# Seven block products in place of eight for the output matrix of a gated feed-forward block

## The chip, the cores and the metric

The kernel runs on one core of one Trainium2 chip. The metric is the device time of one execution in microseconds (us); lower is better. Before the change it is 1617.84 us, the median of three runs (1617.23 to 1620.64). In the profile, PE is the matrix engine (TensorE), PEld its loading of the stationary operand, DVE is VectorE, ACT is ScalarE, POOL is GpSimd and SP the engine that issues most transfers.

## The reference

Two blocks run one after the other, in 32-bit floating point.

```python
# q, k, v: (8 batches, 8 heads, 576 positions, 64)
scores = scale * q @ k^T
scores = where(scores >= max(scores) - tau, scores, -1e9)
attn   = exp(scores - max) / (sum + 1e-9)
x      = (attn @ v)                      # heads side by side: 4608 tokens x 512
g      = x @ w_gate                      # 4608 x 1536
out    = (g * sigmoid(g) * (x @ w_val)) @ w_out      # 1536 -> 512
```

The change concerns the last product, `hidden @ w_out`, in which `hidden` is the gated 4608 x 1536 array.

## The kernel before

The 4608 tokens are cut into units of 256. For a unit, `gate` and `value` form two rows of 128 hidden features at a time on PE (8 matmuls with 256 moving columns each). `value` multiplies them on DVE; `sigmoids` then applies the sigmoid on ACT and the second multiplication on POOL. It does so for three such pairs at a time (`SIG = 3`), so a unit of six pairs needs it twice. A pair lies in a tile `ht` of 128 x 2 x 256: 128 features, two of them side by side, 256 tokens. `output` multiplies the finished tiles with `w_out`, 128 tokens at a time: twelve matmuls with 512 moving columns, in the order of the features, so that the tiles are read from the first to the last.

```python
def value(j, cs, f, hts, gts):
    ps = rows_of_products(j, cs, f, 1, "pv")                                          # PE
    nc.vector.tensor_tensor(out=hts[f // 2][:, :, 0:n], in0=gts[...], in1=ps, op=ALU.mult)   # DVE, L471
    ...
def sigmoids():
    for _, gt, own in unsig:
        nc.scalar.activation(gt, gt, AF.Sigmoid)                                      # ACT, L480
        for x, ht in enumerate(own):
            nc.gpsimd.tensor_tensor(out=ht, in0=ht, in1=gt[:, 2*x:2*x+2, :], op=ALU.mult)    # POOL, L482
    unsig.clear()

def output(tiles):                       # tiles: (unit, 128-token half)
    for (j, lo, hi), i in tiles:
        po = ps_f.tile([P, 512], ...)
        for f in range(NF):              # NF = 12
            if f % OF == 0:              # OF = 3
                if any(u[0] is hts for u in unsig):
                    sigmoids()
            nc.tensor.matmul(po, hts[f//2][:, f%2, i*P:(i+1)*P], wo[:, f, :], ...)    # PE, L497
            ...                          # after the last f: copy on ACT, transfer out
            if f % OF == OF - 1:
                yield OCOST
```

The products of a unit come late: four pieces into the next unit if there is one, and at once if none is ready.

```python
def block():
    late = iter(())
    while True:
        if not ready:
            yield from late              # no next unit yet: the outputs at once
            ...
        unit = ready.popleft()
        for f in range(0, NF, GR):       # GR = 2
            if f == EARLY:               # EARLY = 4
                yield from late
            gate(...);  yield c
            value(...); yield c
        late = output(tiles_of(unit))
```

All of this fills the gaps of the attention part. Attention goes by slots: a batch has four pairs of heads with five slots each. A slot forms scores on PE, takes maxima on DVE, exponentials on ACT, masks them on DVE, and divides by the sums on POOL (`p`, L327). Two slots later DVE transposes the divided `p` in `turn` (L342); the masks of that later slot come after this in DVE's order, and the scores of the slot after it wait for those masks. Between the steps `fill(part)` issues pieces of the feed-forward block, at a rate that `pace` sets. It is the smallest of the averages, taken up to each coming supply of units, of work over slots.

```python
for x, t in enumerate(seg["tiles"]):
    go = scores(seg, t)
    next(go)                 # scores on PE, maxima on DVE, exponentials on ACT
    ...
    next(go)                 # turn(1) and the masks on DVE
    fill(part)
    next(go)                 # exchange of the sums on ACT
    if len(unsig) >= SIG:
        sigmoids()
    fill(part)
    next(go)                 # sums on DVE, the division of p on POOL
    ...
```

The 64 last positions of each batch make two further units of 256 tokens. The first of them is worked in two halves of 128 tokens, one after the second batch and one after the fourth.

Of the kernel before, what the change touches and what calls it, by code (L numbers as in the profile page):

```python
# [2 lines left out]

# [6 lines left out]
F32 = mybir.dt.float32  # L10
# [3 lines left out]
ALU = mybir.AluOpType  # L14
# [4 lines left out]
def kernel(  # L19
# [25 lines left out]

    nc = tc.nc
    P = 128
    B, H, S, D = q.shape  # L50
    NP = H // 2
    DM, DFF = w_gate.shape
    NCC = DM // P
# [8 lines left out]
    NT = SM // P  # L62
    SH = S // 2
    TC = 256
    XB = 6
    NU = SM // TC
    BT = TC // (S - SM)
    NPAIR = B * NP
    TA = 2
    QA = TA * P  # L70
# [3 lines left out]
    const = ctx.enter_context(tc.tile_pool(name="const", bufs=1))  # L74
    ld = ctx.enter_context(tc.tile_pool(name="ld", bufs=1))
    qkp = ctx.enter_context(tc.tile_pool(name="qkp", bufs=2))
    ptp = ctx.enter_context(tc.tile_pool(name="ptp", bufs=2))
    stp = ctx.enter_context(tc.tile_pool(name="stp", bufs=4))
    hp = ctx.enter_context(tc.tile_pool(name="hp", bufs=8))
    gp = ctx.enter_context(tc.tile_pool(name="gp", bufs=5))  # L80
# [22 lines left out]
    make_identity(nc, ident)  # L103
    vall = const.tile([P, 2 * NJ * D], F32, name="vall")

    wgv = const.tile([P, 2, NCC, DFF], F32, name="wgv")
    wo = const.tile([P, NF, DM], F32, name="wo")

    FW = 384
    TW = 2 * FW  # L110
    spare = const.tile([P, 2 * TW], F32, name="spare")


    XW = NCC * TC
    xall = const.tile([P, XB * XW], F32, name="xall")

    hfirst = const.tile([P, NF, TC], F32, name="hfirst")

# [8 lines left out]
    land = wo.rearrange("p f e -> p (f e)")  # L129
    places = [land[:, n * 2 * TW:(n + 1) * 2 * TW] for n in range(NF * DM // (2 * TW))]  # L130
    places += [xall[:, 3 * XW + n * 2 * TW:3 * XW + (n + 1) * 2 * TW] for n in range(2)]
    los = deque(spare[:, n * TW:(n + 1) * TW] for n in range(2))
    for f in range(0, DFF, FW):
        for c in range(NCC):
            wpieces.append((wgv[:, :, c, f:f + FW], [w[c * P:(c + 1) * P, f:f + FW] for w in (w_gate, w_val)],
# [116 lines left out]
    def scores(seg, t):  # L252
        qT, kT, tiles, halved = seg["qT"], seg["kT"], seg["tiles"], seg["halved"]
        if halved and "p" not in seg:
            seg["p"] = ptp.tile([P, 2 * NT + 1, S], F32, name="p")
        q0 = t * P - seg["q0"]
        heads = [slice(h * D, (h + 1) * D) for h in range(2)]
        if t < NT:
            pss = [ps_s.tile([P, 2, 512], F32, name="sc") for _ in range(2)]
            at = [tiles.index(t), len(tiles) + tiles.index(t)]  # L260
        else:
            pss = [ps_s.tile([P, 2, 512], F32, name="sc")]
            at = [tiles.index(t)]
        if halved:
            put = [(pss[h], u, h, q0 + u * D) for u in range(2) for h in range(2)] if t < NT else \
                [(pss[0], h, h, q0) for h in range(2)]
# [200 lines left out]
    def value(j, cs, f, hts, gts):  # L467
        n = cs.stop - cs.start
        per = rows_per(n)
        ps = rows_of_products(j, cs, f, 1, "pv")  # L470
        nc.vector.tensor_tensor(out=hts[f // 2][:, :, 0:n], in0=gts[f // per][:, f % per:f % per + GR, :], in1=ps,  # L471
                                op=ALU.mult)
        if f % per == per - GR:
            unsig.append((hts, gts.pop(f // per), [hts[x][:, :, 0:n] for x in range((f + GR - per) // 2, f // 2 + 1)]))
        if f == NF - GR and cs.stop == TC:
            del xts[j]

    def sigmoids():
        for _, gt, own in unsig:
            nc.scalar.activation(gt, gt, AF.Sigmoid)  # L480
            for x, ht in enumerate(own):
                nc.gpsimd.tensor_tensor(out=ht, in0=ht, in1=gt[:, 2 * x:2 * x + 2, :], op=ALU.mult)  # L482
        unsig.clear()

    SIG = NF // 4
    OF = 3

    def output(tiles):
        for (j, lo, hi), i in tiles:
            hts = hidden[j, lo, hi]  # L490
            po = ps_f.tile([P, 512], F32, name="po", tag="psf")[:, 0:DM]
            for f in range(NF):
                if f % OF == 0:
                    if any(u[0] is hts for u in unsig):
                        sigmoids()
                    need(NCC * DFF // FW + DM // ne * (f * P // FW + 1))
                nc.tensor.matmul(po, hts[f // 2][:, f % 2, i * P:(i + 1) * P], wo[:, f, :],  # L497
                                 start=(f == 0), stop=(f == NF - 1))
                if f == NF - 1:
                    ob = op.tile([P, DM], F32, name="ob")  # L500
                    nc.scalar.copy(ob, po)  # L501
                    kind, at = j
                    if kind == "full":
                        b, u = divmod(at, NU)
                        at = b * S + u * TC + i * P
                        nc.gpsimd.dma_start(out=out[at:at + P, :], in_=ob)  # L506
                    else:
                        for x in range(2):
                            at = (j[1] * BT + lo // D + 2 * i + x) * S + SM
                            nc.gpsimd.dma_start(out=out[at:at + D, :], in_=ob[x * D:(x + 1) * D, :])  # L510
                if f % OF == OF - 1:
                    yield OCOST

    EARLY = 4
    HCOST, OCOST = NCC, OF * DM / TC
    hidden = {}
    ready = deque()

    def tiles_of(unit):

        first, second = (("full", 0), 0, TC), (("full", 1), 0, TC)
        units = [] if unit == first else [first, second] if unit == second else [unit]
        return [(u, i) for u in units for i in range((u[2] - u[1]) // P)]

    def cost(unit):
        return 2 * NF * HCOST * (unit[2] - unit[1]) / TC + len(tiles_of(unit)) * NF / OF * OCOST

    def supply(b):  # L530

        got = [(("full", b * NU + u), 0, TC) for u in range(NU)]
        if b < BT and b % 2:
            got.append((("last", 0), b // 2 * P, (b // 2 + 1) * P))
        elif b >= BT and b % BT == BT - 1:
            got.append((("last", b // BT), 0, TC))
        return got

    left = [0.0]

    def block():
        late = iter(())
        while True:
            if not ready:
                yield from late
                if not ready:
                    yield 0
                continue
            unit = ready.popleft()
            j, lo, hi = unit  # L550
            cs = slice(lo, hi)
            hts, gts = hidden.setdefault(unit, {}), {}
            c = GR * HCOST * (hi - lo) / TC
            for f in range(0, NF, GR):
                if f == EARLY:
                    yield from late
                gate(j, cs, f, hts, gts)
                yield c
                value(j, cs, f, hts, gts)
                yield c  # L560
            late = output(tiles_of(unit))

    pieces = block()
    credit = [0.0]
# [1 line left out]
    def fill(n):  # L566

        credit[0] += n
        while credit[0] > 0:
            c = next(pieces)  # L570
            left[0] -= c
            credit[0] = credit[0] - c if c else 0
            if not c:
                return 0
        return 1

    def start_batch(b):
        def place(n):
            return xall[:, n * XW:(n + 1) * XW].rearrange("p (c t a r) -> p c t a r", c=NCC, a=2, r=G)

        half = XB // 2
        for u in range(NU):
            j = b * NU + u
            while ("full", j - 2 * NU) in xts:
                fill(HCOST)
            xts["full", j] = place(b % 2 * half + u)
        if b % BT == 0:
            xts["last", b // BT] = place(b // BT % 2 * half + NU)

    arenas = [ptp.tile([P, 2 * NT + 1, S], F32, name="p") for _ in range(2)]
    early = list(range(TA))
    rest = list(range(TA, NT + 1))
    flat = [x.rearrange("p n s -> p (n s)") for x in arenas]
    pbufs = deque(arenas[1][:, 2 * x:2 * x + 2] for x in range(2))
    pTbufs = deque(flat[1][:, 2 * x * S:(2 * x + 2) * S] for x in range(2, 4))
    segs = [{"i": i, "tiles": early, "halved": False} for i in range(NP)]
    segs += [{"i": i, "tiles": rest, "halved": False} for i in [NP - 1, *range(NP - 1)]]  # L600
    segs += [{"i": i, "tiles": list(range(NT + 1)), "halved": True} for i in range(NP, NPAIR)]
    assert (2 * KT + 1) * P <= 2 * S and NP + 4 <= 2 * NT
    gains = []
    for n, seg in enumerate(segs):
        seg["gives"] = supply(n // NP - 1) if n % NP == NP - 1 and n >= NP else []
# [27 lines left out]
    def prepare(seg):  # L633

        i = seg["i"]
        if i in kept:
            seg.update(kept[i])
            return
        qr, kr = raws[i]
        kept[i] = None  # L640
        qT = qkp.tile([P, S], F32, name="qT")
        if i < NP:
            kT = arenas[0][:, 4 + i, :]
            rest = flat[0][:, i * (S - QA):(i + 1) * (S - QA)]
            nc.vector.transpose(out=kT, in_=kr)
            nc.vector.transpose(out=qT[:, 0:QA], in_=qr[:, 0:QA])
            nc.vector.transpose(out=rest, in_=qr[:, QA:S])
            kept[i] = {"kT": kT, "qT": rest, "q0": QA}
        else:
            kT = qkp.tile([P, S], F32, name="kT")  # L650
            nc.vector.transpose(out=kT, in_=kr)
            nc.vector.transpose(out=qT, in_=qr)
        seg.update(kT=kT, qT=qT, q0=0)
# [103 lines left out]
```

## Time and profile before

| | |
|---|---|
| Median time | 1617.84 us |
| Span of the profiled execution | 1615.6 us |
| PE busy | 1546.1 us (96%) |
| DVE busy | 996.4 us (62%) |
| POOL busy | 779.7 us (48%) |
| ACT busy | 710.7 us (44%) |
| Attention ends at about | 1410 us |

A busy PE here means that some matmul was under way; matmuls overlap a little at their ends, so rates are better taken from the starts of following groups. A group of instructions in the profile is named by its line in the kernel, its engine and its operation, with the written tile left of the arrow. Every 32-bit matmul leaves two records in this trace, so `x16` stands for eight matmuls. An entry such as `[1.03 <-POOL ht L482]` says that the engine stood idle for 1.03 us before the row and that line 482 on POOL ended the wait.

### The profile page before, as it was taken

Reading aid. Unit: us, or ns where it says so; the run is one execution under the profiler, and the core shown is the slowest. Engines: PE = TensorE matmul, PEld = TensorE weight load, DVE = VectorE, ACT = ScalarE, POOL = GpSimd, SP = SyncE. Lnnn points to the kernel's source line nnn. Section 1 sums busy time; section 2 is a strip of 40 time slices with the busy share of each in tenths; the row PEclk is TensorE's granted clock in tenths of the full one; section 3 lists DMA queues with packets and bytes.
Section 4 is the critical chain, followed back from the end, with each engine's and each line's share of the span. In section 5 each row is a group of like instructions: output and inputs, shape, how many; then the busy total and the mean of one; then the engine's idle time right before and its main releaser. Section 6 shows DMA issues by size and latency. Waiting matters only on the chain.

```text
span 1615.6 us, 30135 instructions
## 1 busy us (share of the span) xinstructions
PE 1546.1 (96%) x11344; PEld 1031.3 (64%) x11344; DVE 996.4 (62%) x3058; ACT 710.7 (44%) x1864; POOL 779.7 (48%) x726
## 2 busy tenths in 40 slices
PE   6898879899999999999999999999999999999998
PEld 4675555357575775657666766676755775577865
DVE  6886877776667766666666767666666677500000
ACT  6776754334444444444444444444444354311110
POOL 3554466554555555455555455554646554511111
PEclk9899989999999999999999999999999999999999
DMA  7541221111111111011111111101111110000000
GB/s 171 139 142 56 77 50 31 43 43 31 37 37 44 31 37 37 19 34 29 31 43 37 37 37 30 44 13 32 31 43 37 37 33 27 1 14 7 7 14 13
DMA packets 176417, 66.84 MB, mean 41 GB/s; under 512 B 159632, under 2 KB 159632, under 8 KB 176272
## 3 DMA queue, kind: packets, MB, share of 16 engines
q1 hardware_dynamic: 173328, 55.47, 15.2%
q0 software_dynamic: 2944, 9.44, 1.7%
q8 instruction: 90, 1.47, 0.4%
q14 instruction: 55, 0.45, 0.1%
HBM read 55.44 MB, written 9.44 MB: 40 GB/s over the span
## 4 chain that ended last, share of the span: by engine, by line
PE 80%; DVE 7%; ACT 2%; issue 1%; POOL 1%; POOLq 0%; DVEq 0%; ACTq 0%
PE po L497 21%; PE pv L451 21%; PE pg L451 21%; PE sc L272 9%; PE xa L409 8%; DVE p L312 2%; DVE mx L292 1%; DVE p L342 1%; DVE mx L247 1%; POOL p L327 1%; ACT p L308 1%; DVE wo L185 0%; ACT L308 0%; DVE wo L183 0%; DVE wo L181 0%
## 5 line engine op out<-in xcount | busy, mean ns | idle before, releaser
L327 POOL TENSOR_SCALAR p<-p,ri 128x288 f32<-128x288 f32 x486 | 479.0, 1001 | 290.6 <-DVE ri L322 248.7
L451 PE MATMUL pg<-xall,wgv 128*128 128x256 f32 (+1 forms) x1824 | 401.8, 373 | 5.6 <-POOL wgv L190 5.6
L451 PE MATMUL pv<-xall,wgv 128*128 128x256 f32 (+1 forms) x1824 | 398.8, 372 | 0.0
L451 PEld LDWEIGHTS pg<-xall,wgv 128*128 128x128 f32 x1824 | 330.6, 191 | 75.2 <-issue 19.4
L451 PEld LDWEIGHTS pv<-xall,wgv 128*128 128x128 f32 x1824 | 330.2, 191 | 59.7 <-issue 13.6
L497 PE MATMUL po<-wo,ht 128*128 128x512 f32 x816 | 364.0, 598 | 1.0 <-POOL ht L482 1.0
L312 DVE SCALAR_TENSOR_TENSOR p<-sc,th,p 128x288 f32<-128x288 f32 (+1 forms) x540 | 258.5, 529 | 57.3 <-ACT p L308 56.4
L497 PEld LDWEIGHTS po<-wo,ht 128*128 128x128 f32 x816 | 151.2, 190 | 192.0 <-issue 182.9
L482 POOL TENSOR_TENSOR ht<-ht,gt 128x512 f32<-128x512 f32 (+1 forms) x108 | 127.9, 1211 | 226.5 <-ACT gt L480 210.9
L308 ACT ACTIVATE p<-sc,nm 128x288 f32<-128x288 f32 (+1 forms) x540 | 236.8, 511 | 0.7
L292 DVE TENSOR_REDUCE mx<-sc 128x2 f32<-128x576 f32 x252 | 179.3, 748 | 73.3 <-PE sc L272 69.9
L471 DVE TENSOR_TENSOR ht<-gt,pv 128x512 f32<-128x512 f32 (+1 forms) x108 | 70.8, 655 | 232.4 <-PE pv L451 227.4
L304 ACT ACTIVATE th<-nm,cut 128x4 f32<-128x4 f32 (+1 forms) x140 | 41.6, 297 | 391.6 <-DVE nm L295 391.5
L272 PE MATMUL sc<-kT,qT 64*32 64x288 f32 x4032 | 170.8, 413 | 27.3 <-DVE p L312 27.1
L342 DVE STREAM_TRANSPOSE p<-p 128x576 f32<-128x576 f32 x252 | 181.3, 753 | 2.2 <-POOL p L327 2.2
L250 ACT COPY sums<-sums 32x4 f32<-32x4 f32 (+1 forms) x560 | 108.5, 194 | 137.4 <-DVE p L312 130.0
L272 PEld LDWEIGHTS sc<-kT,qT 64*32 64x32 f32 x4032 | 66.5, 106 | 120.5 <-issue 93.3
L409 PE MATMUL xa<-p,vall 64*64 64x288 f32 x2016 | 130.6, 409 | 8.7 <-issue 6.3
L409 PEld LDWEIGHTS xa<-p,vall 64*64 64x64 f32 x2016 | 79.2, 134 | 59.8 <-issue 17.0
L465 ACT COPY gt<-pg 128x512 f32<-128x512 f32 (+1 forms) x114 | 64.7, 567 | 112.0 <-PE pg L451 111.5
L506 POOL DMA_DIRECT2D out_dram<-ob x32 | 19.3, 603 | 171.3 <-ACT ob L501 169.0
L247 DVE TENSOR_REDUCE mx<-mx 32x4 f32<-32x4 f32 (+1 forms) x560 | 83.2, 149 | 10.4
(78 smaller groups left out, 962.5 us busy)
## 6 DMA issues: line engine op xcount, KB each, us to landing
vall<-in_v_dram SPq DMA_DIRECT2D x112, 144.0 KB, 3.1
qraw<-in_q_dram SPq DMA_DIRECT2D x128, 72.0 KB, 2.3
kraw<-in_k_dram SPq DMA_DIRECT2D x128, 72.0 KB, 2.7
out_dram<-ob POOLq DMA_DIRECT2D x32, 256.0 KB, 2.4
wo<-in_moe_w_gate_dram SPq DMA_DIRECT2D x16, 384.0 KB, 3.5
wo<-in_moe_w_val_dram SPq DMA_DIRECT2D x16, 384.0 KB, 4.1
xall<-in_moe_w_out_dram SPq DMA_DIRECT2D x6, 768.0 KB, 4.6
wo<-in_moe_w_out_dram SPq DMA_DIRECT2D x2, 768.0 KB, 4.3
```

Of the source, the lines that this page charges most:

```text
L247: nc.vector.tensor_reduce(out=out, in_=in_, axis=AX.X, op=ALU.max)
L250: nc.scalar.copy(out, in_[:, :, 0])
L272: nc.tensor.matmul(ps[g * G:(g + 1) * G, u, 0:SH], qT[hs, col + a * G:col + (a + 1) * G], kT[hs, c * SH:(c + 1) * SH], start=True, stop=True)
L292: nc.vector.tensor_reduce(out=mx[:, 2 * x:2 * x + 2, 0], in_=tile_[:, :, 0:SH], axis=AX.X, op=ALU.max, negate=True)
L308: nc.scalar.activation(ps[x], scs[x], AF.Exp, bias=nm[:, x:x + 1])
L312: nc.vector.scalar_tensor_tensor(out=ps[x], in0=scs[x], scalar=th[:, x:x + 1], in1=ps[x], op0=ALU.is_ge, op1=ALU.mult, accum_out=sm[:, x, ...
L327: nc.gpsimd.tensor_scalar(out=ps[x], in0=ps[x], scalar1=ri[:, x:x + 1], scalar2=None, op0=ALU.mult)
L342: nc.vector.transpose(out=p, in_=p)
L409: nc.tensor.matmul(xa[a][h * D:(h + 1) * D, at:at + n * G].rearrange("d (i q) -> d i q", q=G), vr[rs, h, j, :], p[rs, lo:lo + n, j, :], st ...
L451: nc.tensor.matmul(ps[:, i], wgv[:, mat, c, (f + i) * P:(f + i + 1) * P], x[:, c, cs], start=(c == 0), stop=(c == NCC - 1))
L482: nc.gpsimd.tensor_tensor(out=ht, in0=ht, in1=gt[:, 2 * x:2 * x + 2, :], op=ALU.mult)
L497: nc.tensor.matmul(po, hts[f // 2][:, f % 2, i * P:(i + 1) * P], wo[:, f, :], start=(f == 0), stop=(f == NF - 1))
```

## The change

A unit's output is a product of a 256 x 1536 matrix with a 1536 x 512 matrix. Cut into two by two blocks, it takes eight block products; Strassen's method takes seven, at the price of sums of blocks. Four sums of blocks of `w_out` are formed once on POOL (`sums_of_weights`). The sums of blocks of the hidden array are formed per unit on POOL, in `sigmoids` and in `seven`. The sums of the products go to DVE, with one on POOL. The first two units keep the old `output`. To make room, the two attention buffers `p` overlap by two tiles, with the slots of odd pairs of heads in another order, and the last tokens have one place in place of two. The first of their units is then worked as a whole, after the fourth batch and ahead of that batch's other units.

```diff
     def sigmoids():
-        for _, gt, own in unsig:
+        for hts, gt, own in unsig:
             nc.scalar.activation(gt, gt, AF.Sigmoid)
-            for x, ht in enumerate(own):
-                nc.gpsimd.tensor_tensor(out=ht, in0=ht, in1=gt[:, 2 * x:2 * x + 2, :], op=ALU.mult)
+            for y, (x, ht) in enumerate(own):
+                nc.gpsimd.tensor_tensor(out=ht, in0=ht, in1=gt[:, 2 * y:2 * y + 2, :], op=ALU.mult)
+                if hts["seven"] and x >= NF2 // 2:
+                    x -= NF2 // 2
+                    fs = slice(2 * x, 2 * x + 2)
+                    h11, h21 = hts[x][:, :, 0:P], hts[x][:, :, P:2 * P]
+                    nc.gpsimd.tensor_tensor(out=hs3[:, fs], in0=h11, in1=h21, op=ALU.subtract)
+                    nc.gpsimd.tensor_tensor(out=h21, in0=h21, in1=ht[:, :, P:2 * P], op=ALU.add)
+                    nc.gpsimd.tensor_tensor(out=hs2[:, fs], in0=h21, in1=h11, op=ALU.subtract)
...
+    def sums_of_weights():
+        for f in range(0, NF2, 2):                 # NF2 = 6
+            fs = slice(f, f + 2)
+            for o, x, y in ((ws3, w22, w12), (w12, w12, w11), (ws2, w22, w12), (ws4, w21, ws2)):
+                nc.gpsimd.tensor_tensor(out=o[:, fs], in0=x[:, fs], in1=y[:, fs], op=ALU.subtract)
+            yield 0
+
+    def seven(unit):
+        hts = hidden[unit]
+        if any(u[0] is hts for u in unsig):
+            sigmoids()
+        ...
+        def block_of(y, i):
+            return lambda f: hts[(y * NF2 + f) // 2][:, f % 2, i * P:(i + 1) * P]
+        def product(h, w):
+            ps = ps_f.tile([P, 512], F32, name="po", tag="psf")[:, 0:DM2]      # DM2 = 256
+            for f in range(NF2):
+                nc.tensor.matmul(ps, h(f), w[:, f, :], start=(f == 0), stop=(f == NF2 - 1))
+            return ps
+        ...                                        # add: one tensor_tensor on DVE
+        nc.scalar.copy(o21, product(block_of(1, 1), ws4))
+        yield SCOST
+        nc.scalar.copy(o11, product(block_of(1, 0), w21))
+        for x in range(NF2 // 2):
+            h12 = hts[NF2 // 2 + x][:, :, 0:P]
+            nc.gpsimd.tensor_tensor(out=h12, in0=h12, in1=hs2[:, 2 * x:2 * x + 2], op=ALU.subtract)
+        yield SCOST
+        ps = product(block_of(0, 0), w11)
+        nc.scalar.copy(o12, ps)
+        add(o11, o11, ps)
+        yield SCOST
+        add(o12, o12, product(lambda f: hs2[:, f, :], ws2))
+        yield SCOST
+        add(o22, o12, product(lambda f: hs3[:, f, :], ws3))
+        nc.gpsimd.tensor_tensor(out=o21, in0=o21, in1=o22, op=ALU.add)
+        yield SCOST
+        ps = product(block_of(0, 1), w12)
+        add(o22, o22, ps)
+        add(o12, o12, ps)
+        ...                                        # transfer of the second 128 tokens
+        yield SCOST
+        add(o12, o12, product(block_of(1, 0), w22))
+        ...                                        # transfer of the first 128 tokens
+        yield SCOST
...
+    def outputs(unit):
+        if unit == FIRST:
+            return iter(())
+        if unit == SECOND:
+            return chain(output(FIRST), output(SECOND))
+        return seven(unit)
...
     def supply(b):
-        got = [(("full", b * NU + u), 0, TC) for u in range(NU)]
-        if b < BT and b % 2:
-            got.append((("last", 0), b // 2 * P, (b // 2 + 1) * P))
-        elif b >= BT and b % BT == BT - 1:
-            got.append((("last", b // BT), 0, TC))
-        return got
+        last = [unit_of("last", b // BT)] if b % BT == BT - 1 else []
+        return last + [unit_of("full", b * NU + u) for u in range(NU)]
...
-            late = output(tiles_of(unit))
+            late = outputs(unit)
...
-    segs += [{"i": i, "tiles": list(range(NT + 1)), "halved": True} for i in range(NP, NPAIR)]
+    segs += [{"i": i, "tiles": ([2, 3, 0, 1] if i % 2 else [0, 1, 2, 3]) + [NT], "halved": True} for i in range(NP, NPAIR)]
```

A block `block_of(y, i)` is six of the twelve feature rows (y = 0: the tiles 0 to 2; y = 1: the tiles 3 to 5) and 128 of the 256 tokens.

## Prediction

> **What bounds the kernel now.** I read the page's busy shares first, then its forty slices, then the chain of work that ended last.
>
> ```profile
> PE 1546.1 (96%) x11344; PEld 1031.3 (64%) x11344; DVE 996.4 (62%) x3058; ACT 710.7 (44%) x1864; POOL 779.7 (48%) x726
> ...
> PE   6898879899999999999999999999999999999998
> ...
> PEclk9899989999999999999999999999999999999999
> ...
> PE 80%; DVE 7%; ACT 2%; issue 1%; POOL 1%; POOLq 0%; DVEq 0%; ACTq 0%
> PE po L497 21%; PE pv L451 21%; PE pg L451 21%; PE sc L272 9%; PE xa L409 8%; DVE p L312 2%; DVE mx L292 1%; DVE p L342 1%; DVE mx L247 1%; POOL p L327 1%; ACT p L308 1%; DVE wo L185 0%; ACT L308 0%; DVE wo L183 0%; DVE wo L181 0%
> ```
>
> PE is the bound: from 300 us on it is never idle for long, and the products that the change cuts (`po`) are a fifth of the chain. In the windows view PE is busy 1090.4 of the 1100 us from 300 to 1400. So PE time saved is time saved, but any wait put on PE's in-order path is lost in full. I therefore looked at how close PE runs to its producers. The timeline of PE, ACT and POOL near the end of attention has a telling spot: a unit ends when no next one is ready, and its outputs start at once.
>
> ```profile
> 1389.44 3.62 PE L451 MATMUL pv<-xall,wgv 128*128 128x256 f32 x16
> 1392.99 0.72 PE L272 MATMUL sc<-kT,qT 64*32 64x288 f32 x16
> 1393.63 5.42 PE L497 MATMUL po<-wo,ht 128*128 128x512 f32 x12
> 1400.09 2.84 PE L497 MATMUL po<-wo,ht 128*128 128x512 f32 x6 [1.03 <-POOL ht L482]
> ```
> ```profile
> 1396.76 1.28 ACT L480 ACT_TABLE_LOAD   x1
> 1398.05 1.67 ACT L480 ACTIVATE gt<-gt 128x512 f32<-128x512 f32 x3
> ```
> ```profile
> 1398.76 3.72 POOL L482 TENSOR_TENSOR ht<-ht,gt 128x512 f32<-128x512 f32 x3 [0.59 <-ACT gt L480]
> 1402.47 1.97 POOL L327 TENSOR_SCALAR p<-p,ri 128x288 f32<-128x288 f32 x2
> ```
>
> PE could begin at 1393.63 only because its first six matmuls read tiles 0 to 2, done long before. Tiles 3 to 5 are multiplied on POOL from 1398.76; the sigmoids wait behind this slot's exponentials. PE still lost 1.03 us. Two costs come from the groups by shape:
>
> ```profile
> L482 POOL TENSOR_TENSOR ht<-ht,gt 128x512 f32<-128x512 f32 x96 | 119.5, 1271 | 216.9 <-ACT gt L480 206.3 <-PE sc L272 10.6
> L482 POOL TENSOR_TENSOR ht<-ht,gt 128x256 f32<-128x256 f32 x12 | 8.3, 732 | 9.6 <-PE sc L272 5.0 <-ACT gt L480 4.6
> ```
>
> **What the Trainium skill says.** "TensorE: Matmul & The Clock Gate", in the part on the array and its queues, says that matmuls stay in program order and that only weight loads are pulled ahead, and that the other engines are strictly first in, first out. The 1.03 us wait agrees: PE did not pass to later work. The same page, section "What's actually happening", puts the clock at half after an idle window of some 3.4 us. The trace agrees in kind: 72 records of `xa` take 4.59 us at 567.76, but 6.42 us after an idle time of 6.29 us at 226.09. "GPSIMD Engine Reference", section 3.1, gives about 2.6 cycles an element for a two-input sum at 1.2 GHz; the two rows above give (1271 - 732) / 256 = 2.1 ns, or 2.5 cycles. Sums on POOL are thus not cheap.
>
> **The change part by part.**
>
> *Fewer products.* In the tail eight matmuls of 256 columns take 3.45 us from start to start (1440.18 to 1443.63), 0.4316 us each, all with fresh weights, so short moving operands cost nothing extra. A unit had 24 matmuls of 512 columns in 20.60 us (from 1478.33). It gets 7 x 6 = 42 of 256: 42 x 0.4316 = 18.13 us. Saved: 2.47 us x 16 units = **39.5 us**.
>
> *One unit of last tokens.* Two halves had 24 groups of 1.79 us (518.58 to 520.37), 43.0 us; a whole one has 12 x 3.45 = 41.4 us. Saved: **1.5 us**.
>
> *Sums, beside PE.* POOL gets per unit 9 + 3 + 1 operations of 256 elements: 13 x 0.732 = 9.5 us, x 16 = 152 us, and for the weights 12 x 1.27 = 15 us. From 779.7 it goes to about 947 us, 58%. DVE gets 7 additions per unit of about 0.42 us (its row for 256 elements from PSUM), 47 us in all: 65%. ACT's three smaller copies replace two. No engine becomes the bound by its sum.
>
> *The first product waits.* The first of the seven reads `block_of(1, 1)`, tiles 3 to 5, the last ones finished; and the POOL order is now multiplication, three sums, multiplication, three sums, multiplication. With the times above, at a spot like 1393.63: tile 3 is ready at 1398.76 + 1.27 = 1400.03, tile 4 after 3 x 0.732 + 1.27 = 3.47 more, at 1403.5, tile 5 at 1407.0. Its last two matmuls add 0.86: the product ends at 1407.8 in place of 1396.2, **11.6 us** of idle PE. Where the unit is followed by another, the outputs come four pieces (over 12 us) later and little is lost. Following the changed code, outputs come at once for units 3, 5, 11 and 13 (the last units of four batches) and for the very last unit 15. Units 11 and 13 have a later sigmoid (a full slot's exponentials ahead of it, or the exchange of sums): about 13.5 us. Sum 2 x 11.6 + 2 x 13.5 = **50 us**. The idle clock adds what the `xa` example lost, 1.9 us, to each: **8 us**.
>
> *The tail.* At the end (last `pv` ends near 1588.4) there is no attention. POOL starts at 1586.43 on tile 3; with sums between, tile 5 is ready 3 x 1.27 + 6 x 0.732 = 8.2 us later, at 1594.6, so the first product ends near 1595.5 and not 1591.0: **4.5 us**.
>
> *Later p.* For the other nine units in attention the burst is 3 x 1.27 + 9 x 0.73 = 10.4 us, not 3.8. At 590.13 such a burst stood ahead of the slot's divisions, which ended at 597.8 for a transposition at 600.01: 2.2 us to spare. With 6.6 us more they come 4.4 us late; PE has 1.6 us in hand (masks end at 587.2, next scores at 588.75), so 2 to 3 us are lost, unless an attention product of 4.5 us lies between, as in three windows of five. Nine x 0.4 x 2.5 = **7 to 9 us**.
>
> *Thinner filling.* The unit after batch 1 is half a unit smaller, so `pace` issues less in batches 2 and 3: by my count 5.7 to 6.0 us of filling a slot against 6.4 to 6.7. A full slot lasts at least about 6.7 us from scores to masks (580.52 to 587.2). Full slots with a single piece of 3.45 us and no attention product hold 1.13 + 3.45 = 4.6 us of PE work, so PE idles 2.1 us in each. I count two of them in batches 2 to 7 before and nine after: 7 x 2.1 = about **14 us** of new idle.
>
> *Weights' sums.* Three bursts of 5.1 us each on POOL: about **3 us**. The overlap of `p` adds no wait that I can find: the shared tiles are written in slots after the previous pair's product.
>
> Sum: 1617.8 - 39.5 - 1.5 + 50 + 8 + 4.5 + 8 + 14 + 3 = 1664. Some of these overlap (a stalled PE lets DVE and POOL catch up), so I take 1658.
>
> **The rivals.** *The gain arrives*: sums and sigmoids are hidden, only the products count. For it: POOL has half its time free, and before the change PE waits for POOL only 1.0 us. Against: that measures an order in which old tiles are read first. It would give 1617.8 - 41 + 4.5, about 1581 us. *POOL or DVE becomes the bound*: against it, 58% and 65%; at 1650 us or above its idle time between bursts would have to vanish. *Only the waits at the four ends*, and nothing from later p or thinner filling: 1617.8 - 41 + 58 + 4.5 = 1639 us. *The weight loads of short products bind*: 42 loads replace 24, but gate and value run at this shape at 0.43 us a matmul; nothing lost.
>
> **Range and chances.** The centre lies between the third rival (1639) and the full sum (1664), nearer the sum. The low end, 1622, has stalls of half the reckoned length; the high end, 1682, has every burst late. Two per cent faster (below 1585.5) needs nearly no stall. Two per cent slower begins at 1650.2, below my centre but near it.
>
> **What would show it.** `po` products at 0.43 us a matmul and about 18.1 us of PE per unit; POOL near 58%. In the waits, PE waiting for POOL `ht` of the multiplication for some 45 to 60 us in about a dozen waits, in four clusters, with the granted clock dipping there; `sc` waiting for the masks rising from 27 us to some 50. I would be wrong if the sigmoids of the four ends come earlier than at 1398, if PE's idle time there is taken from idle time elsewhere, or if POOL's sums run faster than 0.73 us.

## The result and the profile after

The changed kernel takes 1684.41 us (median of four runs, 1682.38 to 1686.92) against 1617.53 us: slower by 4.1% (ratio 1.0413, 95% interval 1.0390 to 1.0435). I had put it at 1658 with a range up to 1682. The direction was right, the size was not.

The page of the changed kernel, busy shares, the slices of PE and of its clock, and the chain:

```profile
PE 1546.9 (92%) x11728; PEld 1154.4 (69%) x11728; DVE 1030.6 (61%) x3148; ACT 709.4 (42%) x1874; POOL 942.8 (56%) x940
...
PE   6898779899979999799999999989997999699997
...
PEclk9899989999998999799999999999997999799998
...
PE 69%; DVE 12%; POOL 5%; ACT 3%; issue 2%; DVEq 0%; POOLq 0%; ACTq 0%
```

PE is almost exactly as busy as before (1546.9 against 1546.1 us) although it was given some 41 us less to do. Busy time counts a matmul for as long as it runs, so work at a slow clock looks like more work. The two slice rows dip at about 500, 690, 1270 and 1450 us (at the first of these PE dips in one slice and the clock in the next); before the change neither was below 9 between 325 us and the last slice. The chain has 5% in POOL, where it had 1%.

Two rows of the waits of the changed kernel (who waited for whom: total us, times, longest), and the same two before the change:

```profile
PE po L563 <- POOL ht L495: 47.2, 14, 8.3
PE sc L285 <- DVE pall L325: 46.4, 44, 4.6
```
```profile
PE po L497 <- POOL ht L482: 1.0, 1, 1.0
PE sc L272 <- DVE p L312: 27.1, 23, 3.7
```

Here is one of the four ends, PE and POOL in order of time, and the granted clock by stretches of five microseconds. In the rows of stretches each engine has its busy time and its count, in the order PE, PEld, DVE, ACT, POOL; the number after them is the clock, as a share of full speed:

```profile
488.76 3.62 PE L464 MATMUL pv<-xall,wgv 128*128 128x256 f32 x16
492.31 0.71 PE L285 MATMUL sc<-kT,qT 64*32 64x288 f32 x16
500.86 2.07 PE L563 MATMUL po<-extra,ht 128*128 128x256 f32 x4 [7.83 <-POOL ht L495]
504.36 2.07 PE L563 MATMUL po<-extra,ht 128*128 128x256 f32 x4 [1.43 <-POOL ht L495]
507.87 2.07 PE L563 MATMUL po<-extra,ht 128*128 128x256 f32 x4 [1.43 <-POOL ht L495]
509.74 4.66 PE L563 MATMUL po<-wo,ht 128*128 128x256 f32 x12
```
```profile
499.53 1.27 POOL L495 TENSOR_TENSOR ht<-ht,gt 128x512 f32<-128x512 f32 x1 [2.03 <-ACT gt L493]
...
503.05 1.26 POOL L495 TENSOR_TENSOR ht<-ht,gt 128x512 f32<-128x512 f32 x1
504.27 0.72 POOL L501 TENSOR_TENSOR xall<-ht 128x256 f32<-128x256 f32 x1
505.07 0.72 POOL L502 TENSOR_TENSOR ht<-ht 128x256 f32<-128x256 f32 x1
505.87 0.72 POOL L503 TENSOR_TENSOR xall<-ht 128x256 f32<-128x256 f32 x1
506.55 1.26 POOL L495 TENSOR_TENSOR ht<-ht,gt 128x512 f32<-128x512 f32 x1
```
```profile
490.00:495.00 5.00, 3.03 (x28) 1.93 (x26) 3.18 (x10) 0.78 (x5) 1.44 (x2) 1.00 0.00 0
495.00:500.00 5.00, 0.00 (x0) 0.00 (x0) 3.49 (x12) 3.54 (x7) 2.97 (x4) 0.65 0.58 94
500.00:505.00 5.00, 2.71 (x6) 1.72 (x7) 0.00 (x0) 0.49 (x1) 4.83 (x6) 0.50 0.62 142
505.00:510.00 5.00, 3.57 (x9) 2.40 (x8) 0.00 (x0) 0.02 (x1) 4.70 (x6) 0.50 0.00 0
510.00:515.00 5.00, 5.00 (x36) 3.64 (x43) 0.33 (x2) 1.49 (x6) 2.02 (x4) 0.64 0.00 0
```

The three waits of PE are the three tiles of the first product: each pair of matmuls starts within 0.1 us of the end of one multiplication of POOL, and the three sums lie between two multiplications. The clock goes to half and stays there for the whole product and most of the next; the three short pairs did not raise it. The first product takes from 493.03 to 509.74, 16.7 us in place of 2.6, and the second 4.6: 16.1 us lost at this end. The next two, read in the same way, lost 15.5 and 16.1. At the last end PE waited another 3.75 us for the attention product, which then took 7.3 us in place of 4.6: 22.8 us, of which the kernel before lost 3.4 at the same place (waits of 1.03 and 2.38 us), so 19.4 more. That is 67 us in all. In the tail the first product took 8.2 us (1651.59 to 1659.80) and the next two 7.2 in place of 5.2: 7.6 us.

The other kind of loss is late p. POOL, then DVE, around 1110 us in the changed kernel:

```profile
1113.18 0.72 POOL L503 TENSOR_TENSOR xall<-ht 128x256 f32<-128x256 f32 x1
1113.88 9.84 POOL L340 TENSOR_SCALAR pall<-pall,ri 128x288 f32<-128x288 f32 x10
```
```profile
1115.90 0.78 DVE L355 STREAM_TRANSPOSE pall<-pall 128x576 f32<-128x576 f32 x1 [1.79 <-POOL pall L340]
1117.87 0.78 DVE L355 STREAM_TRANSPOSE pall<-pall 128x576 f32<-128x576 f32 x1 [1.19 <-POOL pall L340]
```
```profile
1114.42 0.67 PE L285 MATMUL sc<-kT,qT 64*32 64x288 f32 x2
1119.64 2.17 PE L285 MATMUL sc<-kT,qT 64*32 64x288 f32 x30 [4.55 <-DVE pall L325]
```

Ten divisions have piled up behind a burst of sums. DVE waits for them before it can transpose and mask, and PE waits for the masks: 4.55 us, and the scores then take 2.17 us where they take 1.2 at full clock.

### The profile page after: what moved, and what is told of

Same layout as the page of the kernel before. It is cut to its first block, busy times and chain, and to the rows that moved or that the text cites. A ratio compares the mean times of both kernels' runs of the same rounds, so it can differ in the third digit from the quotient of the medians.

```text
span 1683.0 us, 31282 instructions
## 1 busy us (share of the span) xinstructions
PE 1546.9 (92%) x11728; PEld 1154.4 (69%) x11728; DVE 1030.6 (61%) x3148; ACT 709.4 (42%) x1874; POOL 942.8 (56%) x940
## 4 chain that ended last, share of the span: by engine, by line
PE 69%; DVE 12%; POOL 5%; ACT 3%; issue 2%; DVEq 0%; POOLq 0%; ACTq 0%
PE pg L464 18%; PE pv L464 17%; PE po L563 17%; PE sc L285 8%; PE xa L422 8%; DVE pall L325 3%; DVE mx L305 3%; DVE pall L355 2%; POOL ht L495 2%; DVE mx L260 1%; PE po L530 1%; POOL ht L502 1%; POOL xall L501 1%; ACT pall L321 1%; POOL xall L503 1%
## 5 line engine op out<-in xcount | busy, mean ns | idle before, releaser
L340 POOL TENSOR_SCALAR pall<-pall,ri 128x288 f32<-128x288 f32 x486 | 480.0, 1004 | 216.3 <-DVE ri L335 181.6
L464 PE MATMUL pg<-xall,wgv 128*128 128x256 f32 x1728 | 399.5, 384 | 5.6 <-POOL wgv L203 5.6
L464 PE MATMUL pv<-xall,wgv 128*128 128x256 f32 x1728 | 398.9, 384 | 0.0
L464 PEld LDWEIGHTS pg<-xall,wgv 128*128 128x128 f32 x1728 | 326.2, 191 | 71.4 <-issue 13.5
L325 DVE SCALAR_TENSOR_TENSOR pall<-sc,th,pall 128x288 f32<-128x288 f32 (+1 forms) x540 | 258.2, 529 | 54.7 <-ACT pall L321 53.8
L495 POOL TENSOR_TENSOR ht<-ht,gt 128x512 f32<-128x512 f32 x102 | 128.3, 1272 | 224.9 <-ACT gt L493 224.9
L321 ACT ACTIVATE pall<-sc,nm 128x288 f32<-128x288 f32 (+1 forms) x540 | 237.3, 512 | 0.8
L285 PE MATMUL sc<-kT,qT 64*32 64x288 f32 x4032 | 180.9, 418 | 46.8 <-DVE pall L325 46.4
L355 DVE STREAM_TRANSPOSE pall<-pall 128x576 f32<-128x576 f32 x252 | 181.8, 755 | 33.4 <-POOL pall L340 33.4
L563 PE MATMUL po<-wo,ht 128*128 128x256 f32 x768 | 184.3, 396 | 0.0
L422 PE MATMUL xa<-pall,vall 64*64 64x288 f32 x2016 | 133.3, 415 | 11.0 <-issue 11.0
L422 PEld LDWEIGHTS xa<-pall,vall 64*64 64x64 f32 x2016 | 82.2, 136 | 58.2 <-issue 20.3
```

Of the source, the lines that this page charges most:

```text
L285: nc.tensor.matmul(ps[g * G:(g + 1) * G, u, 0:SH], qT[hs, col + a * G:col + (a + 1) * G], kT[hs, c * SH:(c + 1) * SH], start=True, stop=True)
L321: nc.scalar.activation(ps[x], scs[x], AF.Exp, bias=nm[:, x:x + 1])
L325: nc.vector.scalar_tensor_tensor(out=ps[x], in0=scs[x], scalar=th[:, x:x + 1], in1=ps[x], op0=ALU.is_ge, op1=ALU.mult, accum_out=sm[:, x, ...
L340: nc.gpsimd.tensor_scalar(out=ps[x], in0=ps[x], scalar1=ri[:, x:x + 1], scalar2=None, op0=ALU.mult)
L355: nc.vector.transpose(out=p, in_=p)
L422: nc.tensor.matmul(xa[a][h * D:(h + 1) * D, at:at + n * G].rearrange("d (i q) -> d i q", q=G), vr[rs, h, j, :], p[rs, lo:lo + n, j, :], st ...
```

## The experiments

Theory: the loss lies in the waits at the four ends and in the tail, with the slow clock after them. Rivals: late p everywhere; thinner filling by the new supply. Each median is of four or more executions; the kernel before, run beside them, had medians of 1616.7 to 1617.7 us.

**Multiplications first.** The three multiplications of a call of `sigmoids` are issued together, the sums after them.

```diff
                 nc.gpsimd.tensor_tensor(out=ht, in0=ht, in1=gt[:, 2 * y:2 * y + 2, :], op=ALU.mult)
-                if hts["seven"] and x >= NF2 // 2:
+        for hts, gt, own in unsig:
+            for y, (x, ht) in enumerate(own):
+                if hts["seven"] and x >= NF2 // 2:
```

> Only the order on POOL is changed: in each call the three multiplications of the hidden tiles come first and the nine sums after them. Theory (PE waits at the four ends of batches and in the tail, because the first product reads tiles 3 to 5 and POOL puts sums between their multiplications): tile 5 is ready 2 x 2.2 us = 4.4 us sooner. At half clock the six matmuls then follow each other in about 5.2 us, so each end is shorter by about 3.6 us, and the tail loses its whole 7 us: 1684 - 14 - 7 = about 1663. Rival (the bursts of sums delay the divisions of p, and this slows attention everywhere): the burst is as long as before, so nothing changes but the tail: about 1677. Rival (the fill is thinner because of the new supply): also only the tail, 1677.

Measured: 1657.01 us (ratio 1.0250, 1.0234 to 1.0265), 27 us less than the change. The same end on PE in this run:

```profile
498.04 5.49 PE L565 MATMUL po<-extra,ht 128*128 128x256 f32 x12 [7.82 <-POOL ht L495]
```

One wait is left of three, as expected; the first is as long as it was. Both rivals expected 1677. From the scores to the start of what follows the stalled work, the four ends are 5.2, 5.8, 5.2 and 4.0 us shorter than in the change, and the tail is 6.2 us shorter: 26 of the 27 us. PE's waits for the masks stay as they were (27.2 us after 300 us, against 28.0). Only the order of POOL's own work was changed, so 27 us of the loss come from where the sums stand in POOL's queue.

**Outputs wait for the next unit.** When no unit is ready, the products are kept until there is one.

```diff
             if not ready:
-                yield from late
+                if final[0] or last in (None, FIRST, SECOND):
+                    yield from late
...                                      # final is set after attention; sigmoids also in the wait for the one place
```

> When no next unit is ready, the seven products wait until the next unit has done its first four pieces, as for all other units (the first two units and the end of the kernel apart). Theory of the waits at the four ends: the idle time and the slow clock there, measured at some 16 us each and 20 in the last, 68 us in all, go; some slots are left without filling for it, about 10 us back: about 1626. Rival of the late p: only what the ends hide goes, and late p would show more: above 1655. Rival of thin filling: the slots without filling make it worse, 1680 or more.

Measured: 1666.75 us (1.0308, 1.0293 to 1.0323), a miss by 40 us. The waits of PE for POOL at the ends went, but others came. The end of attention in this run, on PE, then POOL and DVE:

```profile
1427.84 0.71 PE L285 MATMUL sc<-kT,qT 64*32 64x288 f32 x16
1448.95 7.45 PE L422 MATMUL xa<-pall,vall 64*64 64x288 f32 x72 [20.40 <-issue]
```
```profile
1435.53 1.27 POOL L495 TENSOR_TENSOR ht<-ht,gt 128x512 f32<-128x512 f32 x1 [2.51 <-ACT gt L493]
...
1446.05 1.98 POOL L340 TENSOR_SCALAR pall<-pall,ri 128x288 f32<-128x288 f32 x2
```
```profile
1448.07 0.78 DVE L355 STREAM_TRANSPOSE pall<-pall 128x576 f32<-128x576 f32 x1 [12.84 <-POOL pall L340]
```

Without its outputs a slot at the end of a batch has nothing to fill it, and PE idles 20.4 us for attention's last product. For 12.8 us of these DVE waits for the last two divisions of p, which stand on POOL behind a burst of three multiplications and nine sums (1435.53 to 1446.05). So this is late p once more, and its answer (above 1655) is the one of the three that fits. The products at the ends also fill those slots; taking them away while the sums stand ahead of the divisions is no cure.

**The supply alone, in the kernel before.** The two halves of last tokens become one unit, given after the fourth batch.

```diff
-        got = [(("full", b * NU + u), 0, TC) for u in range(NU)]
-        if b < BT and b % 2:
-            got.append((("last", 0), b // 2 * P, (b // 2 + 1) * P))
-        elif b >= BT and b % BT == BT - 1:
-            got.append((("last", b // BT), 0, TC))
-        return got
+        got = [(("last", b // BT), 0, TC)] if b % BT == BT - 1 else []
+        return got + [(("full", b * NU + u), 0, TC) for u in range(NU)]
```

> The kernel before, with one part of the change alone: the first unit of last tokens is supplied as a whole after the fourth batch, ahead of that batch's other units, not in two halves. Theory of thin filling: batches 2 and 3 get 5.7 to 6.0 us of filling in a slot, not 6.4 to 6.7, and PE idles in thin slots: 1617.5 - 1.5 + 14 = about 1630. Rival (the supply costs nothing, the loss lies in waits that the seven products bring): 1616.

Measured: 1624.99 us (1.0048, 1.0033 to 1.0063): 8 us, where thin filling was to give 12.

**PE kept busy at the ends.** Matmuls that nobody reads fill the wait.

```diff
             for f in range(NF2):
+                if f % 2 == 0 and warm:
+                    n = warm.pop(0)                 # 14, 5, 5 at an end
+                    ...
+                    for _ in range(n):
+                        nc.tensor.matmul(idle, wgv[:, 0, 0, 0:P], wgv[:, 1, 0, 0:DM2], start=True, stop=True)
                 nc.tensor.matmul(ps, h(f), w[:, f, :], start=(f == 0), stop=(f == NF2 - 1))
```

> The changed kernel with 24 unneeded matmuls of 256 columns, read by nobody, ahead of and between the pairs of the first product at the four ends (14, 5 and 5 of them, 10.4 us of PE time at full clock, where PE waited 10.7 us). They keep PE busy while it waits for POOL. Theory that a part of the loss is the slow clock after the wait: the last pair is 1.0 us and the second product 2.0 us shorter at each end, and the attention product after the last end 2.7 us: 1684 - 12 - 3 = about 1669. Theory that only the wait for POOL costs: 1684, unchanged, or a little more where the added matmuls outlast the wait.

Measured: 1674.48 us (1.0353, 1.0335 to 1.0372), 10 us less, though PE was given more to do. At the last end the sigmoids are issued just ahead of the products, so the added matmuls were not placed there; three ends got them. One of these on PE, in order of time (start, length; the rows that write `idle` are the added matmuls):

```profile
492.58 6.31 PE L570 MATMUL idle<-wgv 128*128 128x256 f32 x28
500.48 1.13 PE L571 MATMUL po<-extra,ht 128*128 128x256 f32 x4 [1.58 <-POOL ht L495]
501.44 2.32 PE L570 MATMUL idle<-wgv 128*128 128x256 f32 x10
503.99 1.13 PE L571 MATMUL po<-extra,ht 128*128 128x256 f32 x4 [0.22 <-POOL ht L495]
504.95 2.32 PE L570 MATMUL idle<-wgv 128*128 128x256 f32 x10
507.50 1.13 PE L571 MATMUL po<-extra,ht 128*128 128x256 f32 x4 [0.22 <-POOL ht L495]
508.47 2.75 PE L571 MATMUL po<-wo,ht 128*128 128x256 f32 x12
```

The granted clock was 1.00 from 490 to 515 us. The pairs still start when POOL is done with them, but they take 1.13 us in place of 2.07, and the second product 2.75 in place of 4.66: at one end about 2.8 us less, at three some 8 of the 10 us. The slow clock is a real part of the loss and the smaller one; the waiting itself stays.

**Spread over five slots.** `pace` may use five slots of the next batch, so that a next unit is always there.

```diff
-        lag = 2
+        lag = 5
...                                      # sigmoids also in the wait for the one place
```

> One number of the changed kernel is another: a batch's feed-forward work is spread over the slots up to five slots into the next batch, not two, so that the next unit is always there when one ends and no products start at once before the tail. (The sigmoids are also called inside the wait for the one place of last tokens.) No slot is left without filling, as it was in the run in which the products only waited. Theory of the four ends: their idle time and slow clock, 68 us, go, and slots get a little thinner, 5 us back: about 1621. Rival (the idle time at the ends covers work of attention that must be waited for anyway, as in that run): 1650 or more. Rival (later p everywhere is the larger part): above 1640.

Measured: 1654.44 us (1.0211, 1.0191 to 1.0232), half of what was expected; the answers of both rivals (1650 or more, above 1640) fit. Two rows of the waits of PE in this run, and then the first of the two rows in the run with the sums later (two experiments on):

```profile
PE sc L285 <- DVE pall L325: 64.2, 45, 5.1
...
PE po L563 <- POOL ht L495: 4.2, 2, 2.4
```
```profile
PE sc L285 <- DVE pall L325: 50.3, 41, 3.8
```

The ends are gone (the 4.2 us are the tail), but the wait for the masks has grown from 46.4 to 64.2 us. The reading was that bursts of sums that had fallen into the stalls of the ends now fall among slots; the next two runs bear it out.

**The same, sums left out.** From the second unit with seven products on, the nine sums of hidden blocks on POOL are left out; the products read sums of another unit.

```diff
-                if hts["seven"] and x >= NF2 // 2:
+                if hts["sums"] and x >= NF2 // 2:
```

> As the run before, and the nine sums of blocks per unit on POOL are left out for all units but the first (the products then read sums of another unit; the output is not the reference's). It shows what the bursts on POOL cost once the ends are mended. Theory that bursts delay the divisions of p and so attention: the tail gains 7 us and attention some 10: 17 us below the run before, about 1604. Rival (POOL's sums are hidden in attention): only the tail, 7 us below it.

Measured: 1624.29 us (1.0031, 1.0021 to 1.0041), 30 us less.

**The same, sums later.** `sigmoids` only notes the sums; they are issued after the slot's divisions of p, or after the first product.

```diff
             next(go)                      # sums on DVE, the division of p on POOL
+            sums_of_hidden()
...                                        # and after the first product in seven
```

> As the first run of this group, and the nine sums of a unit come after the slot's divisions of p and not ahead of them, at the latest after the first product. The work is the same. Theory that their place on POOL is what costs: as without the sums, about 1605, the tail included. Rival (sums hidden in attention): only the tail's 7 us, about 1614.

Measured: 1624.02 us (1.0034, 1.0013 to 1.0055): the same as without the sums. These nine sums cost nothing measurable for their length and 30 us for their place: 6 us in the tail, whose first three products take 9.2 us in place of 15.5, and 24 us in attention.

**And the product of tiles 0 to 2 first.**

> As the run before, and the product that reads only tiles 0 to 2 comes first of the seven. Now only the tail begins products at once; there this product covers 2.6 us of the wait for the last tile, and the clock stays up: 2 us below the run before, about 1603. If the tail does not wait any more, the same as it. Either way it should be below the kernel before by 0.5 to 1%.

Measured: 1623.63 us (1.0032, 1.0020 to 1.0045): no difference from the run before, and not below the kernel before. With the sums late the tail hardly waits: 1.1 us in the run before, 0.2 here.

**Less output in the kernel before.** Three of 24 output matmuls per unit are left out, the saving of the change without its means.

```diff
+                end = NF - 1 if j in (("full", 0), ("full", 1)) else NF - 2 - i
+                if f <= end:
-                nc.tensor.matmul(po, ..., start=(f == 0), stop=(f == NF - 1))
+                    nc.tensor.matmul(po, ..., start=(f == 0), stop=(f == end))
```

> The kernel before, with three of the 24 output matmuls left out in the units from the third on (features missing in the sum; the output is not the reference's): 40 us less PE work, the same saving as by seven products, and nothing else: no sums, no other order, no other supply. Theory that PE is the bound throughout, on which my prediction took the 41 us in full: 1617.5 - 40 = about 1578. Rival (attention's own chain from scores to masks sets the pace of many slots once PE has less filling, so that in attention only a part arrives): the three units of the tail give 7.7 us for certain, and attention perhaps half of the other 32: about 1594.

Measured: 1584.24 us (0.9794, 0.9779 to 0.9808): 33.5 us of the 40 arrive. After 300 us PE waits 12.6 us for the masks, where the kernel before waits 8.5; the rest of the missing 6.5 us was not traced. It is the kernel before with a saving of the change's size, and so the mark against which the means of the change are to be counted.

**Seven products in the tail only.**

```diff
-        return seven(unit)
+        return seven(unit) if unit in SEVEN else output(unit)   # the last three units
```

> The changed kernel with seven products only for the last three units, which are worked after attention, the sums after the multiplications and the product of tiles 0 to 2 first; all other units keep the old output. In the tail PE is the only bound and POOL is idle, so 3 x 2.47 = 7.4 us are saved there; the supply of the changed kernel stays, which cost 8 us in the kernel before. Theory that seven products pay where nothing but PE is busy: 1617.5 + 8 - 7 = about 1618. Rival (the loss comes with the seven products anywhere): above 1630.

Measured: 1612.23 us (0.9969, 0.9956 to 0.9982): 5.5 us below the kernel before.

**The order alone, with the ends left.** Sums later and tiles 0 to 2 first, spread over two slots as in the change.

> The changed kernel with its own spreading over two slots, seven products for all units as in the change, but the sums after the divisions of p, and the product of tiles 0 to 2 first. The four ends stay. Their wait is from the scores' end to the end of tile 3's multiplication, some 7.8 us, of which the first product now covers 2.6: 5.2 us and a shorter slow clock, about 8 us an end and not 16; the tail gains 7 us and late p goes: 1684 - 32 - 7 - 8 = about 1637. Rival (order on POOL counts only through the multiplications): as in the run with the multiplications first, 1657.

Measured: 1633.19 us (1.0099, 1.0082 to 1.0116), 51 us less than the change, without a change of spreading. The same end on PE:

```profile
489.54 2.86 PE L571 MATMUL po<-wo,ht 128*128 128x256 f32 x12
497.42 4.54 PE L571 MATMUL po<-extra,ht 128*128 128x256 f32 x12 [5.03 <-POOL ht L495]
```

The first product covers its 2.6 us of the wait, and 5.0 us are left. The second runs at a slow clock. Taken as above, the ends are 9.0, 7.8, 8.0 and 5.5 us shorter than in the change and the tail 7.1: 37 of the 51 us. The other 14 had been lost elsewhere in attention and go with the place of the sums; the product of tiles 0 to 2 first gained nothing in its own run.

**Two slots early, five later.**

```diff
-        lag = 5
+        lag = 2 if n < 3 * NP else 5
```

> As the best run so far (spread over five slots, sums late, product of tiles 0 to 2 first), but up to the third batch of pairs the spreading is over two slots as in the change, since there five slots left some 10 us of work for later. One end, that of unit 3, is back at about 8 us. Theory that early thin filling is what still holds that run at 1624: about 1622 at most, 1615 if the early part counts in full. Rival (filling lost in one place is lost in another): 1624.

Measured: 1627.76 us (1.0064, 1.0049 to 1.0079), above both answers. So the early part is not what holds the run with five slots back. Where the 4 us were lost was not followed up.

**Supply and one place, in the kernel before.**

```diff
         if b % BT == 0:
-            xts["last", b // BT] = place(b // BT % 2 * half + NU)
+            while ("last", b // BT - 1) in xts:
+                fill(HCOST)
+            xts["last", b // BT] = place(NU)
```

> The kernel before with the change's supply and its one place for last tokens, so that some four to six pieces are worked in a row in the fifth batch before attention may go on; no seven products. Theory that the forced stretch takes filling from later slots and so adds to the 7.4 us of the supply alone: about 1630. Rival (the run with seven products only in the tail has both and stands at 1612, so supply and place together cost at most 2 us): about 1619.

Measured: 1619.06 us (1.0015, 1.0008 to 1.0022). Together they cost 2 us; the forced stretch gives back most of what the supply alone took. Why it does was not followed up.

**Seven products in the tail of the kernel before.** Its own supply and both places; the sums lie in attention's buffers, free by then.

> The kernel before with its own supply and both places, and seven products for the last three units alone; the sums of hidden blocks and of the products lie in attention's buffers, which are free by then. PE saves 3 x 2.47 = 7.4 us in a stretch where nothing else is busy, and the sums come after the multiplications: 1617.6 - 7.4 = about 1610. If the sums of weights (15 us on POOL in the first of the three units) or the last tile delay the tail: 1614. If supply and place really cost several us it stands below the run with seven products only in the tail (1612); if not, at it.

Measured: 1611.07 us (0.9959, 0.9944 to 0.9973), 6.2 us below the kernel before. The last unit on PE in this run:

```profile
1584.03 2.75 PE L573 MATMUL po<-wo,ht 128*128 128x256 f32 x12
1586.62 2.75 PE L573 MATMUL po<-extra,ht 128*128 128x256 f32 x12
1589.21 2.75 PE L573 MATMUL po<-wo,ht 128*128 128x256 f32 x12
1591.80 1.89 PE L573 MATMUL po<-extra,p 128*128 128x256 f32 x8
1593.93 3.72 PE L573 MATMUL po<-extra,p 128*128 128x256 f32 x16 [0.24 <-POOL p L502]
```

The products follow each other every 2.59 us; PE waits 0.24 us in all. It is the lowest median of the runs that leave no work out, though not to be told from the 1612.23 of seven products in the tail of the changed kernel.

## Why the prediction was wrong, step by step

The mechanism was right; the sizes of its terms were not. In us, added to the time before:

| Term | Predicted | Measured | By |
|---|---|---|---|
| Fewer products | -39.5 | -33.5 | less output in the kernel before |
| Supply and one place, with the whole unit | +12.5 | +1.8 | both in the kernel before |
| The four ends, slow clock included | +58 | +67 | trace of the change, against full speed |
| The tail | +4.5 | +7.6 | the same |
| Late p | +8 | +14 | the order alone |
| Sums of the weights, and all that is left | +3 | +10 | difference |
| Taken off for overlaps | -6 | 0 | none needed |
| Sum | +40 | +67 | |

The steps that failed are the waits of PE, reckoned too short at the ends, in the tail and for late p; the saving, taken in full; and the discount. That the sum missed by no more is in part luck: the supply was charged 11 us too much.

**Right.** PE is the bound on average; the length of a product (2.59 us) and of the sums (0.73 us) held; POOL at 56% and DVE at 61% bind nothing by their sums (DVE gets six additions per unit, not the seven that I counted). The four ends, the tail, and the pattern of three waits were where I had put them. The runs confirm their causes: the order on POOL (27 us by the multiplications alone) and the slow clock (10 us by keeping PE busy).

**The four ends: 58 us predicted, 67 measured.** The first product was reckoned 11.6 us late at the two plain ends; it was 14.1 at both. POOL began 1.4 us later after the scores than in the example I had read (6.5 us, not 5.1), and the last pair ran at half clock (1.87 us, where I had 0.86). At the other two it was 14.0 and 14.6 us late, where I had 13.5. The slow clock after that was put at 1.9 us (the example gives 1.8) and was 1.4 to 2.1. At the last end the attention product lost more, 3.75 us of waiting (2.38 before the change) and 2.7 us of slow clock, which I had left out. The tail, 4.5 us predicted, took 7.6 because of the clock: the last pair was 1.0 us longer and the next two products 2.0.

**The saving: 39.5 us predicted in full, 33.5 measured**, by the run with less output. PE is the bound on average, but the longer waits for the masks in that run show that slots with little filling are in part bound by attention's own chain, and a saving there does not arrive. I knew of such slots and charged 14 us of them to the supply; supply and place together cost 2 us. The step was half right: the effect exists, but it belongs to the saving.

**Late p: about 8 us predicted, 14 measured.** The mark of 1584.2, with 1.8 for supply and place, 67 for the ends and 7.6 for the tail, gives 1660.8; 24 us are left to 1684.4. The order alone takes 14 of them away. The other 10 stay when the sums come late, and are not explained; the weights' sums, put at 3 us, are among them. The waits of the scores for the masks after 300 us, in the change and then with less output:

```profile
PE sc L285 <- DVE pall L325: 28.0, 29, 4.6
PE sc L272 <- DVE p L312: 12.6, 16, 2.4
```

With the order alone they are 21.3 us. Spread over five slots the place of the sums costs 24 us in attention, not 14, which suggests that the stalls of the ends had hidden part of it.

**The discount.** I took 6 us off because stalls would let other engines catch up. The measured parts need no such discount. This and the undersized terms put the centre 26 us too low; the high end, too, was set from the same terms.

**Still open.** With ends and bursts mended (1624), the change stands 38 us above 1584 + 2. In the last of these runs PE is busy for 1528.4 us against 1509.1 with less output, and idle for 93 against 74: half is idle time, and half busy time that is slow or longer. The order alone stands 47 us above the same mark, of which its four ends make 37 and 10 are the unexplained ones. So by this estimate some 28 of the 38 us come with the spreading over five slots. It removes the waits at the ends and costs most of what they cost. The kernel before was not run with it, so whether it costs this by itself is not shown.

## What to carry to other kernels

When work is cut on an engine that runs in order, ask first which operand the new first instruction needs, and how late it is produced; an order that read the oldest tile first may have hidden the producer. On the producing engine, put what the bound engine waits for ahead of everything else, and count a wait of several microseconds on PE with its slow clock. Use a trick that trades products for sums where only the products' engine is busy: here three units of the tail gave 6 us, and all sixteen lost 67, or 6 with the sums late and the work spread over five slots.

## What the runs showed that I had not expected

The half clock outlasts its cause. After 7.83 us of idle time, three bursts of two matmuls with 1.43 us between them did not raise it: it stayed at 0.50 until about 513.5 us, 5.6 us after the last gap. At the other ends and in the tail it came back 4.5 to 6 us after the last gap. And idle times as short as 2.4 us, shorter than the window of 3.4 us that the prediction quotes, were sometimes enough to slow what followed: the scores at 240.42 in the changed kernel took 3.04 us after an idle time of 2.41 us, not 1.20, at a clock of 0.52 from 242 to 244 us.
